# Half of one unit's V kept in SBUF between two decode layers, with the loads around it rearranged

## The chip, the cores and the metric

The kernel runs on one core of one Trainium2 chip. The metric is the time of one execution on the device in microseconds (us); lower is better. The kernel before took 2563.91 us, the median of three runs. "PE" is the matmul engine, "DVE" the vector engine, "ACT" the scalar engine, and "SP" the engine whose one in-order queue issues nearly every load.

## The reference, cut to what matters

```python
# B=2 (batch), Sq=1, D=576, H=32 heads, Sk=16384 cached keys, Dh=128, F=4608; all bf16
def A(x, k_cache, v_cache, wq, wo):
    q = heads(x @ wq)                                   # one query per (b, h)
    p = softmax((q . k_cache) * Dh ** -0.5)             # 16384 scores per (b, h)
    return merge(p @ v_cache) @ wo
def Bm(x, w1, w2, w3, w4):
    ...                                                 # x1 = x + a constant when S = 1
    return x1 + gelu(layernorm(x1) @ w3) @ w4
x = x + A(layernorm(x)); x = x + Bm(layernorm(x))       # layer 1
x = x + A(layernorm(x)); x = x + Bm(layernorm(x))       # layer 2: the same caches, the same weights
```

There are 64 pairs (b, h); one pair is called a *unit*. A unit has 4.19 MB of K and 4.19 MB of V. Both layers read the same caches, so whatever stays in SBUF from layer 1 need not be loaded again in layer 2. Layer 2 cannot start before layer 1 is done, MLP included.

## The kernel before

SBUF holds one large buffer `buf` of three *places*. A place is 32768 bf16 columns: K of a unit in the lower 16384, V in the upper. All loads go through a queue that is strictly in order. The head of the queue is issued only when every tile that it overwrites is released, and a transfer that has been issued also waits for the last readers of those tiles:

```python
class Arena:
    def pump(self):
        while self.queue:
            keys, p, n, src, sem = self.queue[0]
            under = [t for t in self.live if t["off"] < p + n and p < t["off"] + t["n"]]
            if not all(t["done"] for t in under):
                return                                   # everything behind it waits too
            self.queue.pop(0)
            deps = [o for t in under for r in t["res"] for o in self.s.readers(r)]
            ...
```

Layer 2 walks the units in reverse, so that K and V of the last two units of layer 1 are simply still there. Near the end of each layer the queue holds the MLP weights w3 and w4, then (for layer 2) wq:

```python
    W4_PIECES = (5, 4, 2, 1)          # twelve blocks of w4, 0.44 MB each, in four transfers
    ...
        self.order = [list(range(U)), list(reversed(range(U)))]
        self.kept = set(self.order[0][-self.N_KEEP:])    # N_KEEP = 2
    ...
        def want_w34(l, p, p1):
            base = p * self.place_n
            rows("w3", l, self.w3, base)
            at, a0 = base + (2 * KT - 1) * self.F // 2, 0
            for c, n in enumerate(self.W4_PIECES):
                m = n * self.FJ * D
                if c == 1:
                    at = p1 * self.place_n               # from its second piece on, w4 overlays w3
                ...
                ring.want([("w4", l, c)], at, m, ...)
                at, a0 = at + m, a0 + n
    ...
        for l in range(2):
            wp = 2 - 2 * l                               # w3, w4 of layer 1 lie in place 2
            for i in range(U):
                kv("K", l, i, {(1, 2): (2, 1, 1), (1, 3): (2, 2)}.get((l, i)))
                ...
                t, r = divmod(i - (10 if (l, i) == (1, 10) else 8), 8)
                if r == 0 and 0 <= t < self.n_wo and (l, i) != (1, 8):
                    want_wo(l, t, wp * self.place_n)     # a piece of wo every eight units
            kv("V", l, U - 1, (2, 1, 1))
            want_w34(l, wp, 2)
            if l == 0:
                want_wq(1, 2)
```

The second piece of w4 overlays the first rows of w3, so it can be issued only after the first matmuls of w3. Those need the layer norm of layer 1's result. Meanwhile the DMA queue has what was issued before: the end of w3, and the *first* piece of w4. Those bytes are the *cover*: they keep the DMA engines at work until the next load can be issued.

## Time and profile before

| what | value | view |
|---|---|---|
| time | 2563.91 us, median of 3 | the run's times |
| HBM read | 1097.74 MB | page |
| rate, 20 to 1240 us and 1540 to 2500 us | 431 GB/s | table of windows |
| one V of 4.19 MB | 9.71 us on each engine | completion records |
| chain that ended last | 60% DMA | page |

From the page of the kernel before: the DMA rows of the 40 slices (busy tenths, and GB/s), the instruction fetches among the queues (packets, MB, share), the bytes read, and the shares of the chain of waits.

```profile
DMA  9999999999999999999999999999999999999999
GB/s 410 429 431 432 433 429 432 431 430 433 430 433 432 431 431 432 431 432 432 425 425 428 428 410 430 433 432 429 433 431 431 432 430 433 430 431 433 431 430 387
q8 instruction: 39, 0.64, 0.1%
HBM read 1097.74 MB, written 0.00 MB: 428 GB/s over the span
DMA 60%; issue 16%; DVE 14%; PE 8%; SPq 1%; ACT 1%; ACTq 0%; DVEq 0%
```

The DMA is busy in every slice and moves 431 GB/s in the steady parts. The kernel is bound by its bytes. The one dent inside the run is the 24th slice (410), near 1500 us. From the table of windows (columns: stretch; its length; busy us of PE, its weight loads, DVE, ACT and POOL with counts; the PE clock granted; the mean busy share of the 16 DMA engines; GB/s):

```profile
core 0: us, PE busy (x) PEld busy (x) DVE busy (x) ACT busy (x) POOL busy (x), PEclk, DMA share, GB/s
20.00:1240.00 1220.00, 780.30 (x17258) 731.45 (x17259) 845.28 (x1222) 596.00 (x929) 0.00 (x0) 0.68 1.00 431
...
1284.00:1288.00 4.00, 3.18 (x112) 3.16 (x113) 0.41 (x4) 0.46 (x2) 0.00 (x0) 0.50 1.02 410
1288.00:1292.00 4.00, 1.51 (x57) 1.42 (x54) 1.26 (x4) 0.49 (x2) 0.00 (x0) 0.50 1.02 410
1336.00:1340.00 4.00, 3.44 (x63) 3.28 (x61) 3.90 (x7) 3.28 (x5) 0.00 (x0) 0.74 1.12 471
1340.00:1344.00 4.00, 2.89 (x34) 2.65 (x32) 3.04 (x7) 2.72 (x3) 0.00 (x0) 0.69 1.00 426
...
1494.00:1498.00 4.00, 4.00 (x137) 4.00 (x134) 3.93 (x5) 1.37 (x3) 0.00 (x0) 0.64 0.53 229
1498.00:1502.00 4.00, 2.31 (x19) 1.98 (x18) 3.04 (x9) 1.94 (x2) 0.00 (x0) 0.50 0.68 229
```

At the layer boundary (1284 to 1344 us) the DMA does not rest in the windows shown. Near 1496 us it falls to half its share. The waits of PE name what happens there (columns after the colon: us in total, times, longest):

```profile
PE misc L644 <- DMA buf<-in_A_wo_dram: 11.3, 1, 11.3
```

PE stands still for 11.3 us until a piece of wo has landed, K and V buffers are released late, and the queue runs empty. Finally the timeline of SP's queue (start us, length us, then line, operation, tile, count):

```profile
1287.14 1.95 SPq L443 DMA_DIRECT2D buf<-in_B_w_dram  x3
...
1323.33 2.18 SPq L409 DMA_DIRECT2D buf<-in_A_k_cache_dram  x2
...
1335.01 0.33 SPq L412 DMA_DIRECT2D buf<-in_A_v_cache_dram  x1
```

These are the second and later pieces of w4, then K of layer 2's unit number 3 (the fourth one), then V of that unit.

**How to read completion records.** The Trainium skill ("DMA: Bandwidth & Descriptors", section "Why a DMA increments its semaphore by 16 and not by 1") says that the 16 engines of a transfer finish independently and each reports for itself. This trace agrees: the 16 records of one transfer lie 0.5 us apart at the first weights, 8.0 us just before 1500 us and 1.1 us just after. What a consumer waits for, and what ends the kernel, is the *last* record. I therefore use two numbers for each transfer below: when its last record came, and the *step* from the last record of the transfer before. If the slowest engine lost nothing, the step is the time of the bytes alone (9.71 us for 4.19 MB).

### The profile page before, as it was taken

To read this page: it belongs to the slowest core of one execution; us is meant where nothing else is said; L and a number is where in the kernel's file an instruction comes from. 1 tells how busy PE (TensorE), PEld (TensorE's weight loads), DVE (VectorE), ACT (ScalarE), POOL (GpSimd) and SP (SyncE) were. 2 spreads that over 40 slices of the span, in tenths; PEclk is the share of its full clock that TensorE was granted. 3 is DMA by queue.
4 is the path that set the end of the run, shared out by engine and by line. 5 is a ranking of instruction groups with operands and counts; after the bars stand their busy time and mean duration, and the time that the engine had idled before them with its cause. 6 is when DMAs were issued, how large, how long until landed. Compare 5 with 4: busy or idle time off the path is not lost.

```text
span 2562.0 us, 84308 instructions
## 1 busy us (share of the span) xinstructions
PE 1648.9 (64%) x36813; PEld 1543.0 (60%) x36813; DVE 1756.3 (69%) x2589; ACT 1231.2 (48%) x1941; POOL 1.0 (0%) x12
## 2 busy tenths in 40 slices
PE   5666666666666656666668766666666665666566
PEld 5555665566556656565667665556656655566565
DVE  5676767677666766766658767766766767677664
ACT  4544544454445445544436555444544544454442
POOL 0000000000000000000000000000000000000000
PEclk8666666666666666766666667666766666666666
DMA  9999999999999999999999999999999999999999
GB/s 410 429 431 432 433 429 432 431 430 433 430 433 432 431 431 432 431 432 432 425 425 428 428 410 430 433 432 429 433 431 431 432 430 433 430 431 433 431 430 387
DMA packets 46759, 1098.46 MB, mean 429 GB/s; under 512 B 4916, under 2 KB 6008, under 8 KB 11512
## 3 DMA queue, kind: packets, MB, share of 16 engines
q1 hardware_dynamic: 46712, 1097.76, 99.9%
q8 instruction: 39, 0.64, 0.1%
q14 instruction: 8, 0.07, 0.0%
HBM read 1097.74 MB, written 0.00 MB: 428 GB/s over the span
## 4 chain that ended last, share of the span: by engine, by line
DMA 60%; issue 16%; DVE 14%; PE 8%; SPq 1%; ACT 1%; ACTq 0%; DVEq 0%
DMA buf<-in_A_k_cache_dram 55%; DVE prod L768 12%; PE tps L739 5%; DVE sd L771 2%; DMA buf<-in_B_w_dram 2%; PE misc L787 1%; DMA buf<-in_A_v_cache_dram 1%; DMA buf<-in_A_wo_dram 1%; PE ops L812 1%; DMA buf<-in_A_wq_dram 1%; SPq L426 0%; ACT ktsb L743 0%; SPq L443 0%; PE sps L756 0%; PE misc L644 0%
## 5 line engine op out<-in xcount | busy, mean ns | idle before, releaser
L743 ACT ACTIVATE ktsb<-tps 128x1024 bf16<-128x1024 bf16 x1152 | 1123.5, 1030 | 875.5 <-PE tps L739 869.5
L739 PE MATMUL tps<-ident,buf 128*128 128x128 bf16 x9216 | 915.7, 264 | 608.9 <-DMA buf<-in_A_k_cache_dram 596.4
L739 PEld LDWEIGHTS tps<-ident,buf 128*128 128x128 bf16 x9216 | 738.9, 121 | 636.9 <-DMA buf<-in_A_k_cache_dram 616.4
L771 DVE TENSOR_REDUCE sd<-prod 128x8 f32<-128x1024 bf16 x896 | 1093.0, 1220 | 31.0
L768 DVE TENSOR_TENSOR prod<-buf,qb 128x1024 bf16<-128x1024 bf16 x896 | 610.4, 681 | 11.2 <-DMA buf<-in_A_k_cache_dram 10.3
L812 PE MATMUL ops<-p,buf 128*128 128x1 bf16 x16384 | 460.8, 164 | 68.0 <-DMA buf<-in_A_v_cache_dram 55.4
L812 PEld LDWEIGHTS ops<-p,buf 128*128 128x128 bf16 x16384 | 442.9, 100 | 77.6 <-DMA buf<-in_A_v_cache_dram 64.3
L789 DVE TENSOR_REDUCE small<-misc 128x1 f32<-128x128 f32 x128 | 37.3, 291 | 636.1 <-PE misc L787 636.1
L756 PE MATMUL sps<-qcur,ktsb 128*128 128x1 bf16 x9216 | 395.8, 166 | 108.4 <-ACT ktsb L743 85.4
L756 PEld LDWEIGHTS sps<-qcur,ktsb 128*128 128x128 bf16 x9216 | 349.7, 101 | 166.0 <-ACT ktsb L743 159.7
L723 ACT ACTIVATE qb<-misc 128x128 bf16<-128x128 f32 x130 | 36.1, 278 | 368.5 <-PE misc L720 368.5
L787 PE MATMUL misc<-identS,small 128*128 128x128 f32 x256 | 95.0, 475 | 14.9 <-DVE small L781 14.9
L787 PEld LDWEIGHTS misc<-identS,small 128*128 128x128 f32 x256 | 69.8, 333 | 16.6 <-DVE small L781 16.6
L798 ACT ACTIVATE p<-sps,small 128x72 bf16<-128x72 f32 x128 | 41.4, 323 | 6.7 <-DVE small L789 6.7
L798 ACT ACTIVATE p<-sd,small 128x56 bf16<-128x56 f32 x128 | 44.4, 347 | 0.0
L715 ACT ACTIVATE qcur<-qt 128x1 bf16 (+1 forms) x130 | 29.2, 225 | 19.0 <-DVE qt L651 19.0
L871 PE MATMUL misc<-lpiece,small 128*128 128x16 f32 x28 | 8.5, 385 | 41.9 <-DVE lpiece L869 41.9
L720 PE MATMUL misc<-ident,qcur 128*128 128x128 bf16 x130 | 34.5, 266 | 1.1 <-ACT qcur L715 1.1
L871 PEld LDWEIGHTS misc<-lpiece,small 128*128 128x128 f32 x28 | 7.0, 311 | 44.5 <-DVE lpiece L869 44.5
L777 DVE TENSOR_REDUCE small<-sps 128x1 f32<-128x72 f32 x128 | 28.4, 222 | 0.4 <-PE sps L756 0.2
L798 ACT ACTIVATION_READ_ACCUMULATOR p<-sps,small (+1 forms) x128 | 27.0, 211 | 0.0
L798 ACT ACTIVATION_READ_ACCUMULATOR p<-sd,small (+1 forms) x128 | 26.3, 206 | 0.0
(88 smaller groups left out, 220.4 us busy)
## 6 DMA issues: line engine op xcount, KB each, us to landing
buf<-in_A_k_cache_dram SPq DMA_DIRECT2D x124, 4096.0 KB, 24.3
buf<-in_A_v_cache_dram SPq DMA_DIRECT2D x124, 4096.0 KB, 33.6
buf<-in_B_w_dram SPq DMA_DIRECT2D x8, 1152.0 KB, 31.8
buf<-in_A_wq_dram SPq DMA_DIRECT2D x8, 1024.0 KB, 10.5
buf<-in_A_wo_dram SPq DMA_DIRECT2D x14, 576.0 KB, 34.6
buf<-in_A_k_cache_dram SPq DMA_DIRECT2D x3, 2048.0 KB, 15.6
buf<-in_B_w_dram SPq DMA_DIRECT2D x2, 2160.0 KB, 34.6
buf<-in_A_v_cache_dram SPq DMA_DIRECT2D x2, 2048.0 KB, 22.4
```

Source lines behind the costliest of these rows:

```text
L715: self.act(lambda a, u: a.activation(out=self.qcur[:, q:q + 1], in_=self.qt[:, bass.ds(u, 1)], func=ACT.Copy), r=["qt"], w=[f"qcur{q}"], u ...
L720: self.pe(lambda pe: pe.matmul(self.misc[:, 0:128], lhsT=bcast(self.qcur[:, q:q + 1], 128), rhs=self.ident[:, :], start=True, stop=True), ...
L723: self.act(lambda a: a.activation(out=self.qb[q][:, :], in_=self.misc[:, 0:128], func=ACT.Copy), r=["P:misc"], w=[f"qb{q}"])
L739: ins = pe.transpose(self.tps[b][:, j * 128:(j + 1) * 128], kt[:, (j0 + j) * 128:(j0 + j + 1) * 128], self.ident[:, :])
L743: self.act(lambda a: a.activation(out=self.ktsb[k][:, :, :].rearrange("p a b -> p (a b)"), in_=self.tps[b][:, :], func=ACT.Copy), r=[f"P:t ...
L756: ins = pe.matmul(self.sps[sp][:, col:col + 1], lhsT=self.ktsb[k][:, j, :], rhs=self.qcur[:, sp:sp + 1], start=True, stop=True)
L768: self.dve(lambda v: v.tensor_tensor(out=self.prod[d][:, :, :], in0=k3, in1=bcast_mid(self.qb[q][:, :], self.CH), op=ALU.mult), r=[*res, f ...
L771: self.dve(lambda v: v.tensor_reduce(out=self.sd[q][:, o:o + self.CH], in_=self.prod[d][:, :, :], axis=AX.X, op=ALU.add), r=[f"prod{d}"], ...
L787: self.pe(lambda pe: pe.matmul(self.misc[:, 128:256], lhsT=bcast(self.m[:, q:q + 1], 128), rhs=self.identS[:, :], start=True, stop=True), ...
L789: self.dve(lambda v: v.tensor_reduce(out=self.bias[:, q:q + 1], in_=self.misc[:, 128:256], axis=AX.X, op=ALU.max, negate=True), r=["P:misc ...
L798: self.act(lambda a, u, c0=c0, c1=c1, src=src: a.activation(out=self.p[q][:, c0:c1], in_=src, func=ACT.Exp, bias=self.bias[:, q:q + 1], sc ...
L812: ins = pe.matmul(self.ops[q][:, 0:1], lhsT=vt[:, j * 128:(j + 1) * 128], rhs=self.p[q][:, h * self.TB + j:h * self.TB + j + 1], start=(h ...
```

## The change

The intent is to save 2.1 MB. V of layer 1's very first unit (called x) is loaded in two halves. The second half goes to the top quarter of place 2, where nothing else goes until layer 2, and is not reloaded there. So that x comes third in layer 2, the heads get another order in each layer. To leave that quarter free, w3 (20736 columns) and the first piece of w4 must end below column 24576: the first piece shrinks from five blocks to one. wq of layer 2 now lies over w4's pieces. wo of layer 2 moves to another region, so its first piece is queued two units earlier, which should remove the 11.3 us wait. The diff, cut to its core (names of places and the indexing of q, o and the sums by order are left out):

```diff
-    W4_PIECES = (5, 4, 2, 1)
+    W4_PIECES = (1, 4, 4, 2, 1)
 ...
-        self.order = [list(range(U)), list(reversed(range(U)))]
-        self.kept = set(self.order[0][-self.N_KEEP:])
+        heads = [[*range(4, H), 0, 1, 2, 3], [*range(3, H - 1), 0, 1, 2, H - 1]]
+        self.order = [[h * B + b for h in o for b in range(B)] for o in heads]
+        x = self.order[0][0]
+        assert self.order[1][:3] == [*self.order[0][-2:], x]
+        self.kept = {(kind, u, h) for kind in "KV" for u in self.order[0][-2:] for h in range(2)} | {("V", x, 1)}
 ...
                 for k, n in enumerate(split):
+                    if (kind, u) == ("V", x) and k == 1:
+                        if l == 1:
+                            continue
+                        at = 2 * self.place_n + unit
 ...
-            wp = 2 - 2 * l
+            wp = 2 - l
+            wo_at = wp * self.place_n + unit
 ...
-                t, r = divmod(i - (10 if (l, i) == (1, 10) else 8), 8)
-                if r == 0 and 0 <= t < self.n_wo and (l, i) != (1, 8):
-                    want_wo(l, t, wp * self.place_n)
+                if i % 8 == 0 and 8 <= i <= 8 * self.n_wo:
+                    want_wo(l, i // 8 - 1, wo_at)
 ...
-                want_wq(1, 2)
+                rows("wq", 1, self.wq, [*(third + k * n for k in range(KT - 2)), third + unit, third + unit + n])
 ...
     def q_proj(self, l):
-        self.dve(... one copy of 64 columns of q ...)
+        while i < self.U:   # two or three copies, in the layer's order
```

More of the change, by code (lines that the diff above doesn't have):

```diff
@@ L311, in __init__ @@
         n = self.H - 1 - self.N_MID
-        assert n % self.WO_PIECE == 0 and self.WO_PIECE * 32 == 128
+        assert n % self.WO_PIECE == 0 and self.WO_PIECE * 32 == 128 and self.N_MID == 3
         self.n_wo = n // self.WO_PIECE
-        cuts = [*range(0, n + 1, self.WO_PIECE), self.H - 1]
-        self.wo_cuts = [cuts, [self.H - c for c in cuts]]
         self.s = Sched(nc)
@@ L385, in place @@
         if kind == "K":
-            return (1, 0, 2)[i % 3] if i < self.ROT else (2, 1)[i % 2]
-        return (1, 0, 2)[i % 3] if i < self.ROT - 1 else (1, 2)[i % 2]
+            return (0, 1, 2)[i % 3] if i < self.ROT else (2, 0)[i % 2]
+        return (0, 1, 2)[i % 3] if i < self.ROT - 1 else (0, 2)[i % 2]
     def plan(self):
@@ L391, in plan @@
         unit = 2 * self.half
-        self.order = [list(range(U)), list(reversed(range(U)))]
-        self.kept = set(self.order[0][-self.N_KEEP:])
+        heads = [[*range(4, H), 0, 1, 2, 3], [*range(3, H - 1), 0, 1, 2, H - 1]]
[3 more added lines that the diff above has]
+        self.kept = {(kind, u, h) for kind in "KV" for u in self.order[0][-2:] for h in range(2)} | {("V", x, 1)}
         def kv(kind, l, i, split=None):
             u = self.order[l][i]
-            if l == 1 and u in self.kept:
+            if l == 1 and (kind, u, 0) in self.kept:
                 return
@@ L413, in kv, with rows @@
                           sem=f"{kind}{pl}")
-        def rows(kind, l, w, at, last=None):
+        def rows(kind, l, w, ats):
             n = w.shape[1]
@@ L424, in rows @@
                     ap = w[k * 128:D, :].rearrange("r (c n) -> (r c) n", c=2)
-                ring.want([(kind, l, k)], at + k * n if last is None or k < KT - 1 else last, m,
-                          [lambda e, v, ap=ap: e.dma_start(v, ap)])
-        def want_wq(l, p):
-            rows("wq", l, self.wq, p * self.place_n + unit, last=p * self.place_n + 7 * unit // 8)
+                ring.want([(kind, l, k)], ats[k], m, [lambda e, v, ap=ap: e.dma_start(v, ap)])
         def want_w34(l, p, p1):
             base = p * self.place_n
-            rows("w3", l, self.w3, base)
+            rows("w3", l, self.w3, [base + k * self.F for k in range(KT)])
             at, a0 = base + (2 * KT - 1) * self.F // 2, 0
@@ L458, in want_wo @@
                       sem="wo" if j < self.n_wo else None)
-        want_wq(0, 2)
+        n, third = self.wq.shape[1], 2 * self.place_n
+        rows("wq", 0, self.wq, [third + k * n for k in range(KT)])
         for l in range(2):
-            wp = 2 - 2 * l
+            wp = 2 - l
+            wo_at = wp * self.place_n + unit
             for i in range(U):
                 kv("K", l, i, {(1, 2): (2, 1, 1), (1, 3): (2, 2)}.get((l, i)))
-                if l == 1 and i < self.EARLY:
-                    kv("V", l, i)
-                elif i >= 1 and (l, i - 1) != (1, self.EARLY - 1):
-                    kv("V", l, i - 1)
-                t, r = divmod(i - (10 if (l, i) == (1, 10) else 8), 8)
-                if r == 0 and 0 <= t < self.n_wo and (l, i) != (1, 8):
-                    want_wo(l, t, wp * self.place_n)
+                j = i if l == 1 and i < self.EARLY else i - 1
+                if j >= 0 and (j != i - 1 or (l, j) != (1, self.EARLY - 1)):
+                    kv("V", l, j, {(0, 0): (2, 2), (1, 2): (2, 2)}.get((l, j)))
+                if i % 8 == 0 and 8 <= i <= 8 * self.n_wo:
+                    want_wo(l, i // 8 - 1, wo_at)
                 if i == 8 * self.n_wo + 2:
-                    want_wo(l, self.n_wo, wp * self.place_n + 2 * unit - self.N_MID * D)
+                    want_wo(l, self.n_wo, wo_at + self.half - self.N_MID * D)
                 if l == 0 and i == 1:
-                    want_w2(wp * self.place_n + unit)
+                    want_w2(wo_at + n // 2)
             kv("V", l, U - 1, (2, 1, 1))
@@ L478, in plan @@
             if l == 0:
-                want_wq(1, 2)
+                rows("wq", 1, self.wq, [*(third + k * n for k in range(KT - 2)), third + unit, third + unit + n])
     def wo_piece(self, l, j):
-        return tuple(sorted(self.wo_cuts[l][j:j + 2]))
+        if j == self.n_wo:
+            return 0, self.N_MID
+        h = self.order[l][0] // self.B + j * self.WO_PIECE
+        return h, h + self.WO_PIECE
     def load_wo_last(self, l):
@@ L490, in halves @@
     def halves(self, kind, l, u, h):
-        l = 0 if u in self.kept else l
+        l = 0 if (kind, u, h) in self.kept else l
         keys = [(kind, l, u, h), (kind, l, u, 2)]
@@ L501, in release @@
     def release(self, kind, l, u, h):
-        if l == 1 or u not in self.kept:
+        if l == 1 or (kind, u, h) not in self.kept:
             for k in self.halves(kind, l, u, h):
@@ L650, in q_proj @@
                        lambda w, g, j: w[:, g * 128:(g + 1) * 128])
-        self.dve(lambda v: v.tensor_copy(out=self.qt[:, 1:self.U + 1], in_=self.sps[1][:, 0:self.U]), r=["P:sps1"], w=["qt"])
+        i, o = 0, self.order[l]
+        while i < self.U:
+            n = next(n for n in range(1, self.U) if i + n == self.U or o[i + n] != o[i] + n)
+            self.dve(lambda v, i=i, n=n: v.tensor_copy(out=self.qt[:, 1 + i:1 + i + n],
+                                                       in_=self.sps[1][:, o[i]:o[i] + n]), r=["P:sps1"], w=["qt"])
+            i += n
     def mlp(self, l):
@@ L712, in query @@
     def query(self, l, i):
-        u, q = i if l == 0 else self.U - 1 - i, i % 2
+        q = i % 2
         self.act(lambda a, u: a.activation(out=self.qcur[:, q:q + 1], in_=self.qt[:, bass.ds(u, 1)], func=ACT.Copy),
-                 r=["qt"], w=[f"qcur{q}"], u=u + 1)
+                 r=["qt"], w=[f"qcur{q}"], u=i + 1)
     def query_rows(self, l, i):
@@ L792, in exps @@
     def exps(self, l, i):
-        u = self.order[l][i]
         q = i % 2
@@ L800, in exps @@
                 accum_out=self.lsum[:, bass.ds(u, 1)]),
-                r=[res, f"bias{q}"], w=[f"p{q}", "lsum"], u=2 * u + part)
+                r=[res, f"bias{q}"], w=[f"p{q}", "lsum"], u=2 * i + part)
     def weigh(self, l, i, h):
@@ L819, in weigh @@
             self.dve(lambda v, u: v.tensor_copy(out=self.o[:, bass.ds(u, 1)], in_=self.ops[q][:, 0:1]),
-                     r=[f"P:ops{q}"], w=["o"], u=u)
+                     r=[f"P:ops{q}"], w=["o"], u=i)
     def normalizers(self, u0, u1):
@@ L835, in normalize, with project, f @@
                  r=["den", res], w=["otn"])
-    def project(self, h0, h1, parts):
+    def project(self, i, n, w, res):
         B, D, KT = self.B, self.D, self.KT
         out = self.misc[:, 256:256 + KT * B]
-        for first, n, w, res, after in parts:
-            def f(pe, first=first, n=n, w=w):
-                for j in range(n):
-                    h = first + j
-                    ins = self.d_matmuls(pe, out, w[:, j * D:(j + 1) * D], self.otn[:, h * B:(h + 1) * B],
-                                         j == 0 and first == h0, first + n == h1 and j == n - 1)
-                return ins
-            self.pe(f, r=[*res, "otn"], w=["P:misc"])
-            after()
+        def f(pe):
+            for j in range(n):
+                ins = self.d_matmuls(pe, out, w[:, j * D:(j + 1) * D], self.otn[:, i + j * B:i + (j + 1) * B],
+                                     j == 0, j == n - 1)
+            return ins
+        self.pe(f, r=[*res, "otn"], w=["P:misc"])
         self.add_out(out)
@@ L861, in project_piece @@
         B, D, KT, J = self.B, self.D, self.KT, self.WO_PIECE
-        h0, h1 = self.wo_piece(l, t)
-        u0, u1, n = h0 * B, h1 * B, self.wo_cols
+        n = self.wo_cols
         w, res = self.ring.get(("wo", l, t))
@@ L869, in project_piece @@
         self.dve(lambda v, u: v.tensor_copy(out=self.lpiece[:, :], in_=self.lsum[:, bass.ds(u, 2 * n)]),
-                 r=["lsum"], w=["lpiece"], u=2 * u0)
+                 r=["lsum"], w=["lpiece"], u=2 * n * t)
         self.pe(lambda pe: pe.matmul(dps, lhsT=bcast(self.cone[:, :], 128), rhs=self.lpiece[:, :], start=True,
@@ L876, in project_piece @@
         self.dve(lambda v, u: v.tensor_tensor(out=self.opiece[:, :], in0=self.o[:, bass.ds(u, n)], in1=den, op=ALU.mult),
-                 r=["dpiece", "o"], w=["opiece"], u=u0)
+                 r=["dpiece", "o"], w=["opiece"], u=n * t)
         def rows(pe):
@@ L943, in attention @@
         self.s.tag = None
-        u, h = self.order[l][-1], self.order[l][-1] // self.B
         self.unit_max(l, U - 1)
         self.exps(l, U - 1)
-        h0, h1 = self.wo_piece(l, self.n_wo)
-        u0, u1 = min(h, h0) * B, (max(h, h1 - 1) + 1) * B
-        self.normalizers(u0, u1)
-        self.normalize(u0, u1, self.o[:, u0:u1], "o")
+        mid, last = U - (self.N_MID + 1) * B, U - B
+        self.normalizers(mid, U)
+        self.normalize(mid, U, self.o[:, mid:U], "o")
         self.weigh(l, U - 1, 0)
-        key = ("wo", l, self.n_wo)
-        w, res = self.ring.get(key)
-        self.project(h0, h1, [(h0, h1 - h0, w, res, lambda: self.ring.done(key))])
+        w, res = self.ring.get(("wo", l, self.n_wo))
+        self.project(mid, self.N_MID, w, res)
+        self.ring.done(("wo", l, self.n_wo))
         self.weigh(l, U - 1, 1)
-        q = (U - 1) % 2
-        self.normalize(u, u + 1, self.ops[q][:, 0:1], f"P:ops{q}")
-        self.project(h, h + 1, [(h, 1, self.wolast[:, :], ["wolast"], lambda: None)])
+        self.normalize(U - 1, U, self.ops[(U - 1) % 2][:, 0:1], f"P:ops{(U - 1) % 2}")
+        self.project(last, 1, self.wolast[:, :], ["wolast"])
 def bass_interleave_layers__mha_block_cached__mixer_s_mlp__decode_kernel(
```

## The prediction

> **What bounds the kernel.** The DMA queue throughout. The page's slices show DMA at 9 tenths in all 40; the table of windows gives 431 GB/s from 20 to 1240 us and from 1540 to 2500 us. The Trainium skill ("DMA: Bandwidth & Descriptors", Specifications) gives a fabric ceiling of 435; the trace agrees. The chain of waits is 60% DMA. Compute has slack: a unit's compute takes about 15 us, its 8.4 MB of K and V 19.4 us (landings 9.71 us apart per 4 MB). So time = bytes on the slowest of the 16 DMA engines + that engine's idle time.
>
> **What the change does.**
> 1. 2.1 MB of V (half of one unit) is loaded once instead of twice: 9.71/2 = 4.86 us less on every DMA engine, all on the critical path.
> 2. wo's first piece of layer 2 moves ahead of two units' loads. In the kernel before, PE waits 11.4 us for it (waits view), buffers come free late, and DMA falls to half share from 1494 to 1500 us: 3.3 us of aggregate DMA time in that slice (410 instead of 432 GB/s). I don't book this: the transfers around the dip still land, on their slowest engine, at 1492.6, 1502.2, 1511.9 and 1521.7 us, 9.7 us apart as everywhere. Each transfer has 16 completion records (the skill, same page, "Why a DMA increments its semaphore by 16 and not by 1": engines finish independently); before the dip they lie 8.0 us apart from first to last, after it 1.1. The lead grows by some 1.6 us per round of 16 KB instruction fetches, which hit one half of the engines. So only engines that were ahead idled. The PE wait and the dip will vanish, the time hardly moves (0 to 0.6 us gained).
> 3. w4's first piece shrinks from 2.2 to 0.44 MB; the next overlays w3's first rows, so it waits for their matmuls, as before (issue at 1287.1 us). w3 lands at about 1287.6; 1.06 us of first piece then covers an issue that needs some 2.0 us to flow (read from the restart after the dip): a new gap of about 0.5 us.
> 4. In layer 2 half of V's load is missing before unit 3's loads. Unit 3's V is issued at 1335.0 us and flows at about 1337.3; the data ahead of it would end at 1337.9 on the slowest engine. 0 to 1 us lost.
> 5. Copies of q in pieces, the other head order, the split first V load: nothing measurable.
>
> **Sum.** -4.9 +0.5 +0.2 -0.4 = -4.6: about 2559.2 us. Range 2556.8 to 2561.2 us. Faster by over 2%: 0.005; within 2%: 0.99; slower: 0.005.
>
> **What would show it.** HBM bytes 2.1 MB lower; steady windows still 431 GB/s; no PE wait on wo over 2 us; no half-share window near 1495 us; completion spread near 8 us to the end instead of 1 us; a short DMA dip near 1289 us. If step 2 is wrong and the dip cost 3 us, the time is about 2556. If the new waits exceed 2 us, the gain shrinks toward 0 to 2 us.
>
> **What would make it wrong.** One more instruction fetch on the slowest engine (1.6 us); a new order of waits at the layer boundary, where wq's rows now overlay w4's pieces; the last w4 pieces, which now overlay V of the last unit but one (free at 2525 us, issue near 2543 us).

## The result, and the profile after

| | before | after |
|---|---|---|
| time, median of 6 | 2564.25 us (2563.83 to 2565.33) | 2563.78 us (2562.63 to 2565.01) |
| HBM read | 1097.74 MB | 1095.64 MB |
| rate in the two steady stretches | 431 GB/s | 431 GB/s |

The ratio is 0.9998, with a 95% interval of 0.9986 to 1.0011. Ratios here and below are the mean time of one kernel's fast runs over that of the other's in the same rounds, so not quite the quotient of the medians. The class is "same", which a stake of 4.86 us (0.19%) made all but certain and which says nothing for the prediction; the time lies above the predicted range of 2556.8 to 2561.2 us. Of 4.86 us, half a microsecond arrived by the medians; the ranges of the two kernels overlap, so even this half is not clear of the noise. The profiled run of the kernel after is its slowest (2565.01 us), that of the kernel before an ordinary one (2563.87 us); this matters for the sums below.

From the page of the kernel after, the same lines:

```profile
DMA  9999999999999999999999999999999999999998
GB/s 410 429 431 433 432 430 432 432 431 431 431 431 433 431 432 432 432 430 431 427 378 429 428 433 431 433 431 434 430 431 432 431 433 431 431 433 432 430 431 370
q8 instruction: 39, 0.64, 0.1%
HBM read 1095.64 MB, written 0.00 MB: 427 GB/s over the span
DMA 60%; issue 16%; DVE 15%; PE 8%; ACT 0%; SPq 0%; DVEq 0%
```

The bytes fell as planned, and the dent of the 24th slice is gone (410 became 433). A new dent stands in the 21st slice: 378 instead of 425. A slice is 64 us, so this is 47/431 x 64 = 7.0 us of aggregate DMA time. The windows of the kernel after show where in that slice (same columns as before):

```profile
20.00:1240.00 1220.00, 774.60 (x17252) 719.50 (x17253) 845.62 (x1222) 591.59 (x929) 0.00 (x0) 0.68 1.00 431
...
1284.00:1288.00 4.00, 3.27 (x115) 3.24 (x116) 0.41 (x3) 0.37 (x2) 0.00 (x0) 0.50 0.52 207
1288.00:1292.00 4.00, 1.92 (x66) 1.75 (x64) 1.26 (x4) 0.49 (x2) 0.00 (x0) 0.50 0.94 303
1336.00:1340.00 4.00, 4.00 (x128) 4.00 (x126) 3.93 (x5) 0.86 (x2) 0.00 (x0) 0.50 0.81 307
1340.00:1344.00 4.00, 3.31 (x56) 3.23 (x55) 3.93 (x6) 3.20 (x5) 0.00 (x0) 0.50 0.86 332
...
1494.00:1498.00 4.00, 4.00 (x43) 3.94 (x42) 1.65 (x3) 2.77 (x3) 0.00 (x0) 0.50 0.93 401
1498.00:1502.00 4.00, 3.61 (x69) 3.44 (x68) 3.93 (x5) 3.91 (x9) 0.00 (x0) 0.75 1.03 442
```

The DMA share falls to 0.52 at 1284 to 1288 us and to 0.81 and 0.86 at 1336 to 1344 us. Both are the places that the prediction named. The wait of PE for wo is no longer among the waits. The queue's timeline after, at the same three loads:

```profile
1287.06 1.34 SPq L445 DMA_DIRECT2D buf<-in_B_w_dram  x2
...
1326.90 2.18 SPq L416 DMA_DIRECT2D buf<-in_A_k_cache_dram  x2
...
1338.92 0.33 SPq L419 DMA_DIRECT2D buf<-in_A_v_cache_dram  x1
```

The first is where it was (1287.06 against 1287.14). The other two come 3.6 and 3.9 us later. Why is visible where layer 2's compute starts, in the timeline of DVE. First the kernel before, then the kernel after (in brackets: idle time before, and what ended it):

```profile
1312.15 0.23 DVE L651 CAST qt<-sps 128x64 bf16<-128x64 f32 x1 [6.61 <-PE sps L619]
```

```profile
1315.58 0.36 DVE L659 CAST qt<-sps 128x56 bf16<-128x56 f32 x3 [7.75 <-PE sps L624]
```

The copy of q, with which layer 2 begins, comes 3.43 us later. The extra copies themselves are not it: all three take 0.36 us instead of 0.23.

The completion records of the two profiled runs give the account (times in us; the step is from the transfer before in the queue):

```
data                        before: last (step)   after: last (step)    excess after
w4 first piece              1292.86 (5.25)        1288.56 (1.06)        -
w4 second piece, 1.77 MB    1297.08 (4.23)        1295.42 (6.86)        2.63
last of w4                  1300.22               1302.80               -
wq, fourth rows             1310.17 (2.48)        1313.58 (3.31)        0.83
last of wq                  1311.41               1314.84               -
V of unit 2 (4.2 / 2.1 MB)  1330.96 (9.71)        1329.55 (4.88)        -
K of unit 3, first half     1335.86 (4.90)        1335.86 (6.30)        1.40
K of unit 3, second half    1342.31 (6.45)        1341.02 (5.16)        0.26 (before: 1.55)
V of unit 3                 1352.03 (9.72)        1353.36 (12.34)       2.63
```

V of unit 2 shows the saving: 4.88 us instead of 9.71, so the kernel after saves 4.83 us there. It loses 2.63 + 0.83 + 1.40 + 0.26 + 2.63 = 7.75 us in other steps, where the kernel before loses 1.55 us. Net: 7.75 - 1.55 - 4.83 = 1.37 us later. The table has 1353.36 - 1352.03 = 1.33 us at unit 3's V; the remainder is rounding of many small steps. The two profiled runs as wholes differ by 1.14 us. The median run of the kernel after is 1.2 us shorter than this profiled one. The trace of its repetition (e10 below, 2563.41 us) is closer to a median run: there w4's second piece loses 2.56 us and unit 3 0.85 and 2.11 us, and V of unit 3 lands at 1351.49 us, 0.54 us before the kernel before; its time is 0.46 us below that of the profiled kernel before.

**What an emptied queue costs.** Here are the 16 records of w4's second piece, each as its time behind the first of them:

```
before: 0 .08 .29 .29 .30 .42 1.23 1.24 1.26 1.36 1.51 1.61 1.69 2.94 3.21 3.34
after:  0 .07 .07 .07 .11 .14 .16  .17  .19  .20  .33  .39  .41  .43  .65  1.91
```

In the kernel before, the engines have drifted apart, and most are 1.6 us or more ahead of the last one. In the kernel after they have all run dry and restart together, so the leads are gone, and one engine is at once 1.91 us late. The flow restarts at 1293.51 (first record) - 4.23 (the bytes) = 1289.28 us, 2.22 us after the issue. The slowest engine had run dry at 1288.56. Its loss of 2.63 us is therefore 0.72 us of empty queue and 1.91 us by which the last record trails the first; 0.65 us of that is the spread of the other 15 engines, 1.26 us the one late engine alone. The trace has one packet of an instruction fetch at 1292.7 us, in just this transfer. There are 39 such packets of 16,384 bytes in both kernels. The Trainium skill ("Runtime: NRT & Kernel Launch", section "Instruction fetch mechanics") says that a sequencer refills its instruction memory in blocks of 16 KiB by DMA, "mostly hidden". The size agrees. What this trace adds is that a fetch coincides with one data engine falling back: where the engines were level (the kernel after, e1, e3, e7 and e10), its record came 1.7 to 1.9 us behind the first and 1.2 to 1.5 us behind the next to last.

The kernel before shows both cases, a fall that costs nothing and one that costs time. Seven packets from 1278 to 1328 us do not lengthen a step; the next, at 1336.0 us, stands in the step of unit 3's K that is 1.55 us too long. Up to the dip near 1496 us the last record falls more than 0.2 us behind its bytes only five times, by 1.46, 1.49, 1.55, 1.54 and 1.56 us, each in a transfer in which a packet stands, and these packets are the 1st, 9th, 17th, 25th and 33rd of the 39. The other 30 packets of that time cost the last record no more than 0.2 us each. In all 14 traces, the lags of the 16 engines behind the first, added up, grew by 14 to 16 us over the nine packets from 13 to 107 us, and by -3 to 5 us over the next 1110 us, in which there is none.

### The profile page after: what moved, and what is told of

The parts are those of the page before. It is cut to its first block, busy times and chain, and to the rows that moved or that the text cites. A ratio compares the mean times of both kernels' runs of the same rounds, so it can differ in the third digit from the quotient of the medians.

```text
span 2563.0 us, 83950 instructions
## 1 busy us (share of the span) xinstructions
PE 1645.9 (64%) x36813; PEld 1532.6 (60%) x36813; DVE 1756.7 (69%) x2592; ACT 1226.3 (48%) x1941; POOL 1.0 (0%) x12
## 3 DMA queue, kind: packets, MB, share of 16 engines
HBM read 1095.64 MB, written 0.00 MB: 427 GB/s over the span
## 4 chain that ended last, share of the span: by engine, by line
DMA 60%; issue 16%; DVE 15%; PE 8%; ACT 0%; SPq 0%; DVEq 0%
DMA buf<-in_A_k_cache_dram 58%; DVE prod L778 12%; PE tps L749 5%; DVE sd L781 3%; PE misc L797 2%; DMA buf<-in_B_w_dram 1%; PE ops L821 1%; DMA buf<-in_A_wq_dram 0%; DVE small L799 0%; PE sps L766 0%; PE sps L613 0%; ACT ktsb L753 0%; SPq L431 0%; PE misc L649 0%; PE misc L579 0%
## 5 line engine op out<-in xcount | busy, mean ns | idle before, releaser
L749 PE MATMUL tps<-ident,buf 128*128 128x128 bf16 x9216 | 903.0, 262 | 623.5 <-DMA buf<-in_A_k_cache_dram 612.3
L749 PEld LDWEIGHTS tps<-ident,buf 128*128 128x128 bf16 x9216 | 727.9, 120 | 651.7 <-DMA buf<-in_A_k_cache_dram 631.7
L781 DVE TENSOR_REDUCE sd<-prod 128x8 f32<-128x1024 bf16 x896 | 1093.2, 1220 | 31.0
```

The source lines that it names most:

```text
L749: ins = pe.transpose(self.tps[b][:, j * 128:(j + 1) * 128], kt[:, (j0 + j) * 128:(j0 + j + 1) * 128], self.ident[:, :])
L781: self.dve(lambda v: v.tensor_reduce(out=self.sd[q][:, o:o + self.CH], in_=self.prod[d][:, :, :], axis=AX.X, op=ALU.add), r=[f"prod{d}"], ...
```

## The experiments

All twelve runs gave a correct result. "Before" is the kernel before, run in the same rounds on the same chip. Differences are small beside the intervals: only those of e1, e6 and e12 exclude 1. Of the others, e3, e4, e5, e9 and e11 have ranges that do not overlap with that of the kernel before; e2, e7, e8 and e10 overlap with it. Each kernel has one trace, and those of e2 and e6 to e9 are of the slowest run of their five, that of e12 is of the fastest. My theory: the saved time was given back by two emptied queues, the first at w4's second piece, for want of cover, the second at unit 3, because layer 2 started later and half a V of cover is gone. Rivals: wo's new place costs something; the new order of heads or the q copies cost something; saved bytes do not count in full.

**e1_small_piece: the short first piece alone, in the kernel before.**

```diff
-    W4_PIECES = (5, 4, 2, 1)
+    W4_PIECES = (1, 4, 4, 2, 1)
```

> The kernel before with one edit: w4's first piece is one twelfth of w4 instead of five, nothing else of the change. No byte is saved. Theory A (the small first piece no longer covers the wait for w3's matmuls, the DMA drains at about 1289 us in layer 1's MLP): the landing after the first piece comes 6 to 7 us after it instead of 4.2, the time rises by 2 to 4 us. Theory B (the piece sizes are harmless, the expected 4.9 us went elsewhere, to the head order or the places): no gap near 1289 us, time within 0.7 us of the kernel before.

Measured: 2569.9 us against 2563.98, ratio 1.0023 (1.0010 to 1.0037), so 5.9 us slower, more than the 2 to 4 us that I expected. The step of w4's second piece was 6.87 us, as in the kernel after. The upward miss has its own cause: here wq's first rows overlay w4's last pieces, were issued only at 1302.84 us, and the queue emptied a second time (step 5.50 us instead of 2.49). The windows of this kernel show it:

```profile
1284.00:1288.00 4.00, 3.84 (x131) 3.81 (x132) 0.35 (x3) 0.00 (x0) 0.00 (x0) 0.50 0.57 192
...
1302.00:1306.00 4.00, 1.89 (x27) 1.59 (x24) 1.09 (x7) 0.50 (x2) 0.00 (x0) 0.50 0.50 154
```

The first gap needs neither the new order nor the kept half of V. The second drain is also a clean look at the fetch. After it, the 16 records of wq's first and second rows lie within 0.33 and 0.31 us. A fetch packet stands at 1311.7 us, and the records of the third rows, the last at 1313.99 us, are again level but for one engine, which is 1.67 us behind. That step is 3.84 us, not 2.48.

**e2_wo_alone: wo's new place alone, in the kernel before.**

```diff
-                t, r = divmod(i - (10 if (l, i) == (1, 10) else 8), 8)
-                if r == 0 and 0 <= t < self.n_wo and (l, i) != (1, 8):
-                    want_wo(l, t, wp * self.place_n)
+                t, r = divmod(i - 8, 8)
+                if r == 0 and 0 <= t < self.n_wo:
+                    want_wo(l, t, wp * self.place_n + l * unit)
```

> The kernel before with one edit: wo's first piece of layer 2 goes to the free V region of its place and two units earlier in the queue. Theory A (only DMA engines that were ahead idled in the dip at 1494 us): the PE wait of 11.4 us for wo and the dip are gone, the completion spread stays near 8 us to the end, the time is within 0.7 us of before. Theory B (the dip cost 3 us): the time falls by about 3 us.

Measured: 2563.31 us (2563.11 to 2563.68) against 2563.98, ratio 0.9998 (0.9984 to 1.0011). The wait of PE for wo is gone, and so is the dip, as its windows show:

```profile
1494.00:1498.00 4.00, 4.00 (x65) 3.94 (x64) 3.19 (x5) 3.66 (x5) 0.00 (x0) 0.63 1.03 442
1498.00:1502.00 4.00, 2.65 (x58) 2.10 (x55) 3.93 (x5) 4.00 (x10) 0.00 (x0) 1.00 0.95 410
```

An 11.3 us wait and a dip to half share were removed for 0.7 us at most. At the end of the run the records now lie 8.31 us apart; in the kernel before, 1.65 us. The dip had only taken time from engines that were ahead.

**e3_no_half_v: the kernel after, with the half of V loaded again in layer 2.**

```diff
-        self.kept = {...} | {("V", x, 1)}
+        self.kept = {...}
 ...
-                        if l == 1:
-                            continue
```

> The changed kernel with the half of V loaded again in layer 2 (2.1 MB more), everything else as changed. Theory A (the 4.9 us were saved, but the drained queue near 1289 us and the compute start that it delays cost as much): the gap near 1289 us stays, the gaps before unit 3's K and V in layer 2 are filled by the extra load, and the time is 2 to 4 us above the kernel before, so less than 4.9 us above the changed one. Theory B (bytes do not count, something else bounds): the same time as the changed kernel. Theory C (bytes count in full and nothing else matters): 4.9 us above the changed kernel.

Measured: 2566.51 us (2565.72 to 2566.68) against 2563.98, ratio 1.0010 (0.9996 to 1.0023), so some 2.5 us slower than before, with the same bytes. From its windows:

```profile
1284.00:1288.00 4.00, 3.55 (x121) 3.52 (x122) 0.41 (x3) 0.12 (x1) 0.00 (x0) 0.50 0.55 197
1336.00:1340.00 4.00, 4.00 (x107) 4.00 (x105) 3.93 (x7) 1.12 (x3) 0.00 (x0) 0.50 0.96 401
```

The first gap stays (last records at 1288.27 and 1295.02 us, a step of 6.75). Unit 3 loses nothing: its K halves and V step by 4.91, 4.87 and 9.69 us, although V is issued at 1337.99 us, 3.0 us later than in the kernel before. So the gap at w4 costs about 2.5 us (a net figure: it also holds wo's new place, and where single engines fall back in the rest of the run), and the second loss arises only when the half V is missing. The kernel after stands 0.5 us below before, this one 2.5 above: leaving out 2.1 MB gained 3.0 us of the 4.85, so about 1.8 us went at unit 3.

**e4_pieces: the kernel after with twice the cover.** Two blocks of w4 still fit below the kept quarter. The second piece is halved too, so it waits for fewer matmuls.

```diff
-    W4_PIECES = (1, 4, 4, 2, 1)
+    W4_PIECES = (2, 2, 3, 2, 2, 1)
```

> The changed kernel with w4 in pieces (2, 2, 3, 2, 2, 1): the first is twice as large, the second overlays w3's first row block alone and so waits for one block of matmuls instead of two. Theory A: the step to the second piece's landing near 1292 us has no idle time (2.1 to 2.6 us for 2.1 us of data), layer 2's first unit starts about 3 us earlier than in the changed kernel, the time falls to 2559 to 2561.5 us. Theory B (piece sizes harmless): the time stays at 2563.8 us.

Measured: 2561.11 us (2560.89 to 2561.81) against 2563.98, ratio 0.9990 (0.9976 to 1.0004), so 2.9 us below before. The kernel after, each against its own before, is 0.5 to 0.65 us below (first result and e10), so e4 gains 2.2 to 2.4 us on it. It changes two things, more cover and an issue 1.5 us earlier, and does not tell them apart. From its windows and its queue's timeline:

```profile
1284.00:1288.00 4.00, 3.58 (x127) 3.56 (x128) 0.41 (x3) 0.09 (x1) 0.00 (x0) 0.50 0.92 330
1288.00:1292.00 4.00, 1.96 (x68) 1.80 (x66) 1.26 (x4) 0.49 (x2) 0.00 (x0) 0.50 0.97 377
1336.00:1340.00 4.00, 3.30 (x58) 3.22 (x56) 3.93 (x7) 3.11 (x4) 0.00 (x0) 0.63 0.90 303
```

```profile
1285.57 3.63 SPq L445 DMA_DIRECT2D buf<-in_B_w_dram  x4
...
1335.82 0.33 SPq L419 DMA_DIRECT2D buf<-in_A_v_cache_dram  x1
```

The share at 1284 to 1288 us is 0.92 instead of 0.52; the second piece's step is 2.05 us, what its bytes take, and the third's 3.89 instead of some 3.17. V of unit 3 is issued 3.1 us earlier than in the kernel after, because layer 2 starts earlier. Its step is still 12.36 us: the data ahead of it land earlier as well (1336.89 instead of 1341.02 us), so its own gap stays. The later start of layer 2 is thus not what makes this gap.

**e5_pieces_split_v3: e4, and V of unit 3 in two halves**, so that its first half need not wait for the whole region.

```diff
-  kv("V", l, j, {(0, 0): (2, 2), (1, 2): (2, 2)}.get((l, j)))
+  kv("V", l, j, {(0, 0): (2, 2), (1, 2): (2, 2), (1, 3): (2, 2)}.get((l, j)))
```

> The changed kernel with w4 in pieces (2, 2, 3, 2, 2, 1), as in the run before, and with unit 3's V of layer 2 loaded in two halves, so that its first half waits for the first half of unit 0's V alone (1.7 us of matmuls less). Theory A (what is left of the loss lies at unit 3's V, whose buffer comes free too late): its idle time of 1 to 2 us shrinks, the time falls a further 0.7 to 1.7 us, to 2559.4 to 2560.4 us. Theory B (the rest is instruction fetches or the head order): 2561.1 us as without the split.

Measured: 2561.4 us (2561.26 to 2562.89) against 2564.04, ratio 0.9991. The split alone gave nothing over e4.

**e6_all_three: e5, and one more chunk of the first unit's scores on PE** instead of DVE, so that layer 2's first unit ends sooner.

```diff
-        return self.NCH // 2 + 1
+        return self.NCH // 2 + (2 if (l, i) == (1, 0) else 1)
```

> As the run before, and unit 0 of layer 2 scores ten of its sixteen chunks on TensorE instead of nine, six instead of seven on VectorE, whose dot products (1.86 us each) end that unit. Theory A: unit 3's K and V are issued some 1.8 us earlier, no idle time is left there, the time is 2558.8 to 2560 us, near the 2559.1 us that 2.1 MB less would give alone. Theory B: no further change.

Measured: 2560.13 us (2558.61 to 2561.7) against 2564.04, ratio 0.9983 (0.9969 to 0.9996). This is 3.9 us below before, of the 4.86 that the bytes allow, and just above the 2558.8 to 2560 us that I expected.

**e7_first_unit: that edit of the first unit alone, on the kernel after.**

> The changed kernel with the edit of unit 0 of layer 2 alone (ten chunks on TensorE): the drain near 1289 us stays as it is. Theory A (the second half of the loss is set by when unit 0 of layer 2 is through): unit 3's V is issued some 1.8 us earlier and the time falls by 1 to 2 us, to about 2562.3 us. Theory B (everything is lost at 1289 us, the later gaps only echo it): the time stays at 2563.8 us.

Measured: 2563.27 us (2562.18 to 2564.96) against 2564.04, ratio 0.9995. I expected 1 to 2 us less than the kernel after; it was 0.1 to 0.5 (against e10 and the first result, which are of other rounds). The mechanism moved as meant but by little: V of unit 3 was issued at 1337.53 instead of 1338.92 us, and its step was 10.66 instead of 12.34. That a step 1.7 us shorter shows as 0.5 us at most makes this run inconclusive.

**e8_quarter_v: keep a quarter of V, not a half**, so that four blocks of w4 fit as cover.

```diff
-    W4_PIECES = (1, 4, 4, 2, 1)
+    W4_PIECES = (4, 4, 3, 1)
-        self.kept = {...} | {("V", x, 1)}
+        self.kept = {...} | {("V", x, 2)}       # V of x in pieces of 2, 1 and 1 quarters; the last is kept
```

> The changed kernel with only a quarter of V kept (1.05 MB instead of 2.1 MB saved), which leaves room for w4 in pieces (4, 4, 3, 1). Theory A (saved bytes count in full wherever the DMA queue does not drain): the first piece of w4 covers 4.2 us, no idle time near 1289 us, unit 3's loads in layer 2 have 2.4 us more data ahead of them and do not drain either; the time is 2.4 us below the kernel before, 2561 to 2562 us, and so below the changed kernel, which saves twice the bytes. Theory B (the loss belongs to the head order or to keeping a part of V at all): no gain over the kernel before.

Measured: 2563.68 us (2563.28 to 2566.36) against 2564.06, ratio 0.9998. I expected 2561 to 2562, so this is a miss. The gap at w4's second piece was gone (step 4.22 us). But the longer pieces of w4 now held up what overlays them:

```profile
1298.62 4.43 SPq L431 DMA_DIRECT2D buf<-in_A_wq_dram  x5
```

wq's first rows had to wait for the matmuls of w4's second piece, were issued at 1298.62 us, and stepped by 6.03 us instead of 2.5. The gap had moved one transfer on. V of unit 3 lost time as well (step 11.59 us instead of 9.71).

**e9_pieces_first_unit: e4 and the edit of e7, without the split.**

> The changed kernel with w4's pieces (2, 2, 3, 2, 2, 1) and ten chunks of unit 0 of layer 2 on TensorE, without the split of unit 3's V, which by itself gave nothing. Theory A (both waits shortened is what counts): 2559.5 to 2561 us. If the split mattered after all: above 2561 us.

Measured: 2561.16 us (2560.12 to 2561.9) against 2564.06, ratio 0.9987 (0.9974 to 1.0001), just above the 2559.5 to 2561 that I expected, and no better than e4. V of unit 3 stepped by 10.95 us, less than in e4, but the first half of its K by 6.92.

**e10_changed_again: the kernel after, unedited**, as a control in the same rounds as e8 and e9.

> The changed kernel itself again, on the same chip and in the same rounds as the two before, for direct comparison: 2563 to 2565 us.

Measured: 2563.41 us (2562.9 to 2563.96) against 2564.06, ratio 0.9998 (0.9984 to 1.0011). The result repeats. So do the steps: w4's second piece 6.79 us, unit 3's first half of K 5.75, its V 11.82. The spread within the second piece is again level but for one engine (0.73 us, then 1.91), with a fetch packet at 1292.3 us.

**e11_quarter_v_wq: e8 with its moved gap closed as well.** w4's second piece is halved, and wq's rows are placed over regions that are free earlier.

```diff
-    W4_PIECES = (4, 4, 3, 1)
+    W4_PIECES = (4, 2, 2, 3, 1)
-   rows("wq", 1, self.wq, [*(third + k * n for k in range(KT - 2)), third + unit, third + unit + n])
+   rows("wq", 1, self.wq, [third + at for at in (unit, unit + n, 2 * n, 3 * n, unit + 2 * n)])
```

> As the quarter of V before, with the drain that its trace showed taken away: there the queue ran dry at wq's first rows (6.0 us to their landing instead of 2.5), which overlay w4's second piece and waited for its matmuls. Now w4 is in pieces (4, 2, 2, 3, 1) and wq's first two row blocks lie over w3's last rows and w4's first piece. Theory A (saved bytes count in full where nothing drains): no step between landings at the layer boundary is more than 0.7 us above its data's time, the time is 2561 to 2562.3 us, 2.4 us below the kernel before. Theory B (keeping a part of V gains nothing by itself): 2563 us or more.

Measured: 2561.54 us (2561.31 to 2561.69) against 2564.11, ratio 0.9990 (0.9976 to 1.0004). This is 2.57 us less, for 1.05 MB less, which take 9.71/4 = 2.43 us. Its windows at the same places:

```profile
1284.00:1288.00 4.00, 3.27 (x111) 3.24 (x112) 0.41 (x3) 0.37 (x2) 0.00 (x0) 0.50 1.01 405
1288.00:1292.00 4.00, 1.74 (x58) 1.60 (x55) 1.26 (x4) 0.49 (x2) 0.00 (x0) 0.50 1.02 414
1336.00:1340.00 4.00, 3.38 (x62) 3.30 (x60) 3.93 (x6) 3.17 (x5) 0.00 (x0) 0.50 1.02 397
```

The DMA rests in none of them, and by the medians the saved bytes count in full. (At unit 3 a step of K is 1.04 us too long, with a packet at 1336.7 us; in the kernel before it is 1.55.) The new order of heads, the copies of q and wo's new place are all in this kernel, so they cost nothing that these runs can see. The records show the leads too: after w4's second piece they lie 3.28 us apart, not 1.9.

**e12_all_three_again: e6 once more**, in the rounds of e11.

> The fastest version so far (w4 in six pieces, unit 3's V in two halves, ten chunks of unit 0 on TensorE) again, next to the run above on one chip: 2558.6 to 2561.7 us as in its first five runs, below the kernel before by 3 to 4 us.

Measured: 2560.09 us (2559.11 to 2560.62) against 2564.11, ratio 0.9984 (0.9971 to 0.9998). It is the fastest version found, 4.0 us below before, twice. At unit 3 the DMA no longer rests in the first of the two windows:

```profile
1336.00:1340.00 4.00, 2.50 (x41) 2.42 (x41) 3.93 (x6) 1.35 (x3) 0.00 (x0) 0.50 1.00 430
```

The four halves of unit 3 (K, K, V, V) still step by 5.02, 5.80, 5.63 and 4.75 us, 1.8 us more than their bytes (2 x 9.71), while the records drift from 0.77 to 2.43 us apart: the kernel again pays for delays of single engines after they were made level. It is still within 2% of the kernel before: the whole stake was 0.19%.

## Why the prediction was wrong

1. **Bound, bytes, saving: right.** The read fell by 2.1 MB, the steady rate stayed at 431 GB/s, V of unit 2 took 4.88 instead of 9.71 us. e11 shows, by its medians, that saved bytes are worth their full time when nothing runs dry.
2. **Step 2 (wo and the dip): right.** The wait and the dip vanished, and e2 prices both at 0 to 0.7 us. The half-share dip was worthless because only engines with a lead were idle. One sign failed: a spread near 8 us to the end came in e2 (7.7 to 8.3 us), but in the kernel after it is 5.7 to 5.9 us, since its drains had taken the leads.
3. **Step 3 (w4's first piece): right in mechanism and place, wrong in size.** The prediction put w3 landed plus the first piece at 1287.6 + 1.06 = 1288.66 us; it was 1288.56. The issue was put at 1287.1 and came at 1287.06; the flow was put 2.0 us later, and came 2.2 us later. So the empty queue itself was nearly as predicted, 0.72 us against 0.5. But the step lost 2.63 us. This is the step that failed: the +0.5 of the sum priced the gap at its empty time alone. The term left out is what happens *after* the restart: the engines are level, so the one that falls back, to 1.91 us behind the first, ends the transfer late. The prediction knew that leads hide losses, since step 2 rests on it, and did not ask what an emptied queue does to them. It did list "one more instruction fetch on the slowest engine (1.6 us)" among what would make it wrong, which is close to what the records show, and that the gain would shrink to 0 to 2 us if the new waits exceed 2 us; it booked neither. e1 and e3 show this gap (steps of 6.87 and 6.75 us), e1 without the rest of the change; e3 and e4 price it at 2.2 to 2.5 us.
4. **Step 4 (unit 3): the same term is missing.** The prediction took "Unit 3's V is issued at 1335.0 us" from the profile before, as if the compute of layer 2 would start when it did. It starts when wq has landed, 3.4 us later (1314.84 instead of 1311.41), and that V was issued at 1338.92 us. But the data ahead of it also came later, at 1341.02 instead of the predicted 1337.9 us, so this error cost little: reckoned as for w4, V flowed from 1350.66 - 9.71 = 1340.95 us, just before the slowest engine was through. In e4 V is issued at 1335.82 us, near the 1335.0 of the prediction, and steps by 12.36 us all the same. The wait of the slowest engine was thus within the predicted 0 to 1 us (none here, 0.3 us in e10, 0.9 in e4); what cost is again the engines that fall back behind the level rest. The steps of unit 3 lost 1.40 + 0.26 + 2.63 = 4.29 us in this run, where the kernel before lost 1.55. In medians the extra loss is about 1.8 us (e3), where the sum had +0.2.
5. **Step 5 (order of heads, q copies): right**, by e11 and by the 0.36 us of the copies.
6. **Sum in medians:** -4.85 (bytes) + 2.5 (first gap, e3) + 1.8 (unit 3, after less e3) = -0.5 us; the measured difference of the medians is -0.47. The -0.4 of the prediction for wo's new place is inside the second term. The second and third term come from differences of medians, so the sum closes by construction. The independent check is e4: closing most of the first gap was worth 2.2 to 2.4 us.

The fear that the prediction listed as "wq's rows now overlay w4's pieces" was not what hit the kernel after, where wq's first rows stepped by 2.64 us. It did hit e1 and e8.

**What stays open.** That the fetch *causes* the late engine is argued, not shown: the two come together in time in every trace, with the counts given above, but no run moved a fetch by itself. In the kernel after, the fetch packets near unit 3 (1327.1, 1338.5 and 1344.7 us) fit the two late engines of its V (2.04 and 2.70 us, all others within 0.32), but which packet met which engine the trace does not tell, and how much of the lateness belongs to the restart itself is not settled. Nor is it settled why e5, e7 and e9 gave nothing singly while e6 gave 1 us more than e4. The last microsecond that e6 and e12 leave unsaved lies at unit 3 by the steps of e12, but what causes those steps was not tested.

## What to carry to other kernels

Before you shorten a load that depends on nothing, add up how long the loads already issued keep the DMA at work, and compare it with when the next, dependent load can be issued plus its start-up (here 2.0 to 2.2 us); e8 shows that a gap closed at one transfer may open at the next. Judge a DMA-bound kernel by the last completion of each transfer, not by the mean share: a dip at half share cost under 0.7 us while the step with a drain of 0.7 us on the slowest engine lost 2.6, which I put down to the leads, in which small delays hide, being erased by a full drain. Carry every delay on to what it releases, on both sides: here the issue at unit 3 and the data ahead of it moved together, and only their distance mattered.

## What the Trainium skill lacked or had wrong

- "DMA: Bandwidth & Descriptors", section "Where 436 GB/s comes from", says that for transfers from HBM to SBUF the HBM side (about 358 GB/s) binds. With one core running, these runs sustain 431 GB/s for 1220 us on end, close to the page's fabric ceiling of 435. A note under the same page's table of measured rates does say that the other core was idle for its 425, and the skill says as much elsewhere, so it is only this sentence that lacks the condition.
- Same page, Specifications: a first-byte latency of about 0.6 us for loads issued from the sync engine. Reckoned back from the first completion record at the full rate, the data flowed 2.22 us (w4's second piece) and 2.03 us (V of unit 3) after the issue began. That figure includes the completion's own way, so the two are not the same quantity; for the question "how much cover does a dependent load need", 2.0 to 2.2 us is the one to use here. What the page lacks is such a figure for loads from the sync engine; it has one for loads issued from GpSimd.
- Same page, section "Why a DMA increments its semaphore by 16 and not by 1": it says that engines finish independently but not how far apart, or that the distance lasts. In the kernel before it was 0.5 us at the start and 8.0 us at 1490 us, carried from transfer to transfer; a drain erased it in the kernel after (3.33 us before it, 0.65 us for 15 of 16 engines after).
- "Runtime: NRT & Kernel Launch", section "Instruction fetch mechanics": crossing a 16 KiB boundary is "mostly hidden". No page says that a fetch may cost the data transfers time. Here there are 39 packets of 16,384 bytes in each run of before and after; where the engines were level, one of them came 1.7 to 1.9 us behind the first in the transfer in which the packet stands, and in the kernel before every eighth packet up to 1496 us cost the last record 1.46 to 1.56 us and the others at most 0.2 (link argued, not shown).
